# A hand-ordered linear-attention and gated-MLP kernel: three kinds of copies may go to GpSimd, and the written order of all steps is replaced

## The chip, the cores and the metric

The kernel runs on one core of a Trainium2 chip. The metric is the device time of one execution in microseconds (us), as a median of repeated runs; lower is better.

## The reference, cut to what matters

A linear attention with a per-channel decay feeds a gated MLP in float32:

```python
for t in range(S):                       # q, k, v, alpha: (4, 8, 768, 48)
    state = alpha[:, :, t, :, None] * state + np.einsum('bhd,bhe->bhde', k[:, :, t], v[:, :, t])
    y[:, :, t] = np.einsum('bhd,bhde->bhe', q[:, :, t], state)
x = y.transpose(0, 2, 1, 3).reshape(B * S, H * D)      # (3072, 384)
g = x @ w_gate                                         # (384, 1536)
silu = g * (1.0 / (1.0 + np.exp(-g)))
out = (silu * (x @ w_val)) @ w_out                     # (3072, 384)
```

The weights arrive as 64-bit floats.

## The kernel before

**Attention.** The 4 x 768 time steps are cut into 16 units of 192 steps (`u` = 0 to 15; four units are a batch). A unit's loads are alpha, k and q (`La`, `Lk`, `Lq`) and v (`V`). Units 0 to 3 are turned on TensorE (`Ta`, `Tk`, `Tq`, after a widening copy `pa`, `pk`, `pq`), later ones by VectorE's transpose (`tr`, `tk`, `tq`). Then come two scans (`G` backward, `f` forward), k and q multiplied by them (`mk`, `q`), a copy of a part of q (`qc`, line 470, "odd queries") and of v (`vc`, line 476), the scores on TensorE (`S`) and their causal mask on VectorE (`ma`), k turned (`K` with copies `kc` for units 0 to 3, `kr` on VectorE later), the carried state (`B`, or `Bw`, a whole sum with 96 matmul instructions instead of 48), its advance (`ad`), a decay (`de`), and the output (`Y`). Its rows are split in an upper and a lower part (`yh`, `yl`) and moved to the MLP's layout: by TensorE (`R`, `x`) for units 0 and 1, by ten DMAs on the SP queue (`xr`) from unit 2 on.

**MLP.** Eight blocks of 384 tokens, twelve slices of 128 hidden channels each: 96 steps `s`. Each step has three products of nine 128x384 matmuls: `g` (gate), `v` (value) and `o` (out). A float32 product is made of upper and lower parts, so that each factor exists twice. Between them: `sl` (silu, ScalarE, line 700), `h` (times the value product, VectorE, line 704), `hh` (upper part, ScalarE, line 708), `hl` (lower part, line 713, VectorE or GpSimd). There is one PSUM bank for `g` and one for `v`: product `v` of a step starts when `h` of the step before has read the bank. Steps 0 to 6 are block 0, 7 to 13 block 1 (tokens of units 2 and 3), both with the first seven slices.

**Weights.** 19 groups and a last one are loaded as raw 64-bit words (`wl`), cut to float32 by three VectorE operations (`w#v0` to `w#v2`, lines 148, 151, 154), copied as an upper part (`w#a`, line 321) and subtracted for a lower part (`w#p`, line 325). Range checks of all weights follow later (`wr`, `wc`), and those of alpha (`Lc`, `ck`).

**What sets the order.** A string `ORDER` names every step once with its engine: `t` TensorE, `v` VectorE, `s` ScalarE, `g` GpSimd, `y` SP. Each engine runs its own steps in that order, and waits only for the data and the buffers that a step needs. `3+` and `1*` are dummy matmuls on TensorE (lines 766 and 762), which fill waits of the early part. Digits after `@` are PSUM banks.

```python
for word in ORDER.split():
    e, name = word.split(":")
    if name[-1] in "*+":
        (dummy32 if name[-1] == "+" else dummy)(int(name[:-1]))
    else:
        name, *banks = name.split("@")
        todo.pop(name)(engines[e], *(BANKS[int(x)] for x in "".join(banks)))
```

Of the kernel before, what the change touches and what calls it, by code (L numbers as in the profile page):

```python
# [48 lines left out]
s:kc1.0 t:Ta2@45 v:w3v0 s:ad0.2 t:Y0@36 v:q1 y:wl9 v:de1 s:ea2 t:S1@02 v:w4v0 s:yh0.0 v:G2 y:wl10 s:kc1.2 s:vc1 v:w4v1
s:qc1 s:yh0.1 y:wl11 v:w4v2 t:Bw1@1 v:f2 y:wl12 t:Ta3@45 s:ad1.1 v:ma1.1 g:pq2 s:ad1.0 v:ma1.0 v:yl0.1 y:V2 s:ad1.2  # L50
g:pk2 v:yl0.0 v:ma1.2 t:2+ t:Tq2@01 t:R0.1@2 v:w3v1 s:cq2 t:Tk2@36 v:w3v2 s:x0.1 t:Y1@01 v:mk2 g:q2 s:w4a t:R0.0@2
s:yh1.0 t:K2.0@3 s:yh1.1 v:yl1.0 t:K2.2@6 g:w4p s:qc2 v:yl1.1 t:K2.1@0 s:ea3 v:x0.0 t:R0.2@1 y:V3 t:R1.0@2 s:kc2.1
t:S2@45 v:G3 s:x1.0 s:kc2.2 s:kc2.0 t:R1.2@0 v:f3 s:w3a t:R1.1@2 s:x1.2 s:vc2 t:2* t:B2@0 y:Lq3 v:ma2.2 g:w3p s:x1.1
y:La4 s:x0.2 v:ma2.0 t:2* t:g0 v:ma2.1 v:w5v0 y:Lk3 v:w5v1 y:wl13 t:v0 s:sl0 v:w5v2 y:wl14 s:pq3 v:w6v0 t:g1 s:w5a
y:wl15 v:w7v0 v:w6v1 y:wl16 t:Tq3@12 s:sl1 v:w6v2 y:wl17 s:cq3 v:w7v1 s:pk3 v:w7v2 s:w6a y:Lk4 t:2+ t:Tk3@12 v:de2
s:w7a v:mk3 g:w5p v:ad2.0 t:1+ t:2* t:K3.1@1 v:ad2.1 t:K3.2@2 g:w7p s:kc3.1 t:K3.0@3 v:ad2.2 s:kc3.2 y:wl18 v:h0
s:kc3.0 t:2* t:Y2@01 s:hh0 v:de3 v:w8v0 t:v1 s:vc3 y:V4 v:w8v1 s:yh2.0 v:w8v2 s:yh2.1 t:g2 v:yl2.0 g:q3 s:w8a v:h1
v:yl2.1 t:v2 s:hh1 v:hl0 s:qc3 t:S3@01 v:tr4 g:hl1 s:sl2 y:xr2 g:w8p t:g3 v:h2 v:ma3.0 v:tk4 t:Bw3@2 s:sl3 g:w6p
v:ma3.2 v:ma3.1 t:o0 s:ad3.0 v:w9v0 s:ad3.1 v:w10v0 v:w11v0 t:o1 y:La5 s:hh2 v:w11v1 v:w9v1 t:Y3@01 y:Lq4 v:w9v2
v:w10v1 t:v3 s:w9a y:V5 s:yh3.0 v:w10v2 s:vc4 t:g4 v:yl3.0 g:hl2 s:w10a v:h3 v:w9p s:hh3 t:v4 s:sl4 v:w10p s:yh3.1  # L60
t:o2 v:yl3.1 g:hl3 v:h4 y:xr3 v:w12v0 t:o3 v:w12v1 s:hh4 v:w13v0 t:g5 v:w12v2 v:w11v2 t:v5 s:sl5 v:G4 s:w12a t:g6
s:w11a v:h5 g:hl4 s:hh5 t:v6 v:w11p s:sl6 v:w14v0 t:o4 v:h6 g:hl5 v:f4 t:g7 s:hh6 t:v7 s:sl7 v:w14v1 v:w14v2 t:g8 v:h7
g:hl6 t:v8 v:w12p s:sl8 v:w13v1 t:o5 v:h8 v:w15v0 t:o6 v:w15v1 s:hh7 v:w13v2 t:g9 s:hh8 v:w15v2 s:ot6.0 s:ot6.1
y:os6.0 v:mk4 t:v9 s:w14a y:os6.1 v:kr4.0 g:hl7 s:w15a g:hl8 s:sl9 v:kr4.3 s:w13a t:g10 v:kr4.2 g:w13p s:ot6.2 v:kr4.1
s:sl10 t:o7 y:os6.2 g:w14p v:tq4 t:o8 v:h9 y:Lk5 v:w15p t:v10 s:hh9 v:w16v0 v:q4 t:g11 v:w16v1 s:qc4 t:S4@01 v:w17v0
v:w16v2 t:B4@2 v:ma4.2 g:hl9 s:w16a v:h10 g:w16p v:ma4.1 s:sl11 t:v11 s:hh10 v:ma4.0 s:ad4.0 v:tr5 t:g12 g:hl10 y:wl19
v:ad4.1 y:Lq5 t:o9 v:h11 s:sl12 v:G5 t:v12 s:hh11 v:f5 t:g13 v:h12 g:hl11 t:o10 v:tk5 s:sl13 t:v13 s:hh12 v:w18v0
y:La6 v:w18v1 t:g14 v:h13 g:hl12 v:ad4.2 t:o11 s:sl14 v:de5 v:w18v2 t:o12 s:hh13 v:w17v1 v:w17v2 t:Y4@01 v:mk5 s:w18a
# [15 lines left out]
t:o28 s:hh29 v:tk9 g:hl29 t:S8@01 t:B8@2 v:ma8.2 v:f9 t:o29 s:ad8.0 y:La10 t:v30 v:ma8.0 y:Lq9 v:ad8.1 v:ad8.2 t:g31
v:h30 v:de9 s:hh30 t:v31 s:sl31 v:hl30 v:mk9 t:g32 v:h31 v:kr9.1 s:hh31 t:v32 s:sl32 v:kr9.3 t:g33 v:hl31 v:h32
v:kr9.0 t:o30 s:sl33 v:tq9 t:v33 s:hh32 g:hl32 v:kr9.2 y:Lk10 t:g34 v:h33 v:ma8.1 t:o31 v:q9 s:sl34 v:tr10 s:qc9
t:S9@01 s:hh33 t:B9@2 v:G10 y:Lq10 t:o32 v:ma9.0 v:f10 t:v34 t:g35 v:ma9.1 v:h34 v:ma9.2 s:hh34 t:v35 v:hl33 v:hl34
s:sl35 v:ad9.0 t:o33 v:ad9.1 v:h35 t:o34 v:ad9.2 s:hh35 v:hl35 t:g36 v:tk10 t:v36 g:mk10 y:La11 s:sl36 t:g37 v:h36
# [5 lines left out]
t:g43 v:ma10.1 g:hl42 y:wr0 v:kr11.2 y:wr1 t:v43 y:wr2 s:sl43 v:kr11.3 v:ma10.0 t:g44 v:h43 v:f11 t:v44 s:sl44 v:tq11
t:g45 t:o41 v:h44 g:q11 y:Lk12 v:kr11.0 t:o42 v:ad10.0 s:hh43 g:hl43 s:wc0 v:ad10.1 t:v45 v:ad10.2 s:wc1 y:wr3 v:de11
t:o43 s:qc11 v:kr11.1 y:wr4 s:wc2 v:tr12 t:Y10@01 s:sl45 y:wr5 s:hh44 v:h45 g:hl44 y:Lq12 t:g46 v:tk12 s:vc11 s:yh10.0
y:V12 t:v46 v:G12 s:sl46 s:yh10.1 s:hh45 t:g47 v:h46 g:hl45 v:yl10.1 v:yl10.0 t:o44 v:mk12 s:wc3 y:La13 v:f12 t:o45
s:hh46 s:wc4 y:wr6 t:v47 v:tq12 s:wc5 y:wr7 t:S11@01 s:sl47 y:wr8 v:hl46 y:xr10 v:h47 t:B11@2 v:ma11.1 s:hh47 t:g48
# [997 lines left out]
```

## Time and profile before

| | |
|---|---|
| median of 3 runs | 585.48 us (585.07 to 588.24) |
| profiled execution | 588.15 us, span of its instructions 586.4 us |
| TensorE (PE) busy | 557.2 us, 95% of the span |
| VectorE (DVE) busy | 399.4 us, 68% |
| ScalarE (ACT) busy | 256.2 us, 44% |
| GpSimd (POOL) busy | 134.6 us, 23% |
| mean granted TensorE clock | 0.994 |

The span runs from the first to the last instruction; the profiled execution's own time is 1.75 us longer. Busy shares are averages over an early part, in which the attention and the weights are made, and a long part in which TensorE multiplies without a stop.

### The profile page before, as it was taken

The page shows a single profiled execution, that of the slowest core. Times are in us where ns is not written, and L with a number is a line of the kernel's source. Part 1 is how long each engine was busy: PE and PEld are TensorE (multiplying, and loading weights), DVE is VectorE, ACT ScalarE, POOL GpSimd, SP SyncE. Part 2 cuts the span into 40 slices and gives each one's busy share as a digit, 9 for nine tenths or more (in the row PEclk, how much of TensorE's full clock was granted, in tenths as well). Part 3 has the DMA queues.
Part 4 walks back from the last instruction along what each step waited for, and adds up shares of the span by engine and source line. Part 5 has one row for each costly group of instructions (what it writes and reads, how often), then busy time and mean ns, then how long its engine had stood idle before and what let it go on. Part 6 is the DMA issues. An engine that isn't in the chain of part 4 may idle for free.

```text
span 586.4 us, 13722 instructions
## 1 busy us (share of the span) xinstructions
PE 557.2 (95%) x5502; PEld 527.4 (90%) x5502; DVE 399.4 (68%) x625; ACT 256.2 (44%) x591; POOL 134.6 (23%) x130
## 2 busy tenths in 40 slices
...
GB/s 207 292 362 161 312 115 97 40 85 68 144 143 133 122 127 112 122 78 100 87 136 216 193 172 210 227 142 123 220 106 119 72 184 81 60 41 41 0 1 47
DMA packets 95368, 77.67 MB, mean 132 GB/s; under 512 B 32832, under 2 KB 92224, under 8 KB 95296
## 3 DMA queue, kind: packets, MB, share of 16 engines
...
## 4 chain that ended last, share of the span: by engine, by line
PE 69%; DMA 12%; DVE 12%; SPq 3%; issue 3%; ACT 1%; DVEq 0%; ACTq 0%
PE v L692 21%; PE ops L724 21%; PE g L692 21%; DMA raw<-in_moe_w_out_dram 3%; DMA raw<-in_moe_w_gate_dram 3%; DMA raw<-in_moe_w_val_dram 2%; DVE K L505 2%; PE y L619 2%; DVE t L154 1%; PE A L553 1%; DVE h L704 1%; DMA L<-in_q_dram 1%; PE s L530 1%; DMA V<-in_v_dram 1%; DMA Le<-in_k_dram 1%
## 5 line engine op out<-in xcount | busy, mean ns | idle before, releaser
L692 PE MATMUL v<-xT,w 128*128 128x384 f32 x864 | 169.1, 340 | 6.3 <-DVE h L704 6.3
L692 PE MATMUL g<-xT,w 128*128 128x384 f32 x864 | 168.2, 338 | 1.9 <-DMA xT<-X 1.8
L692 PEld LDWEIGHTS v<-xT,w 128*128 128x128 f32 x864 | 151.4, 189 | 9.7 <-DVE h L704 8.8
L724 PE MATMUL ops<-w,hh 128*128 128x384 f32 x576 | 157.8, 337 | 0.0
L692 PEld LDWEIGHTS g<-xT,w 128*128 128x128 f32 x864 | 151.2, 188 | 3.7 <-issue 1.7
L713 POOL TENSOR_TENSOR hl<-h,hh 128x384 fp32r<-128x384 f32 x66 | 73.0, 1108 | 332.1 <-ACT hh L708 327.8
L704 DVE TENSOR_TENSOR h<-h,v 128x384 f32<-128x384 f32 x96 | 53.1, 553 | 115.3 <-PE v L692 108.6
L708 ACT CAST hh<-h 128x384 fp32r<-128x384 f32 x96 | 49.1, 512 | 146.4 <-PE ops L724 85.5
L724 PEld LDWEIGHTS ops<-w,hh 128*128 128x128 f32 x576 | 105.2, 188 | 0.7
L724 PE MATMUL ops<-w,hl 128*128 128x384 f32 x288 | 96.8, 336 | 0.4 <-DVE hl L713 0.4
L700 ACT ACTIVATE h<-g 128x384 f32<-128x384 f32 x96 | 47.0, 490 | 106.4 <-PE g L692 97.3
L505 DVE STREAM_TRANSPOSE K<-Gs 32x384 f32<-32x384 f32 x96 | 54.7, 570 | 2.9 <-PE A L553 1.2
L724 PEld LDWEIGHTS ops<-w,hl 128*128 128x128 f32 x288 | 54.1, 188 | 0.7 <-DVE hl L713 0.7
L713 DVE TENSOR_TENSOR hl<-h,hh 128x384 fp32r<-128x384 f32 x30 | 16.7, 559 | 26.7 <-ACT hh L708 26.4
L448 DVE TENSOR_TENSOR_SCAN AT<-AT,back 128x771 f32<-128x771 f32 x16 | 32.4, 2025 | 0.6
L325 POOL TENSOR_TENSOR w<-t,w 128x768 fp32r<-128x768 f32 (+1 forms) x14 | 26.4, 1903 | 24.0 <-ACT w L321 20.3
L563 DVE TENSOR_TENSOR X<-s,mask 64x384 f32<-64x384 f32 (+1 forms) x48 | 26.2, 553 | 4.2 <-PE s L530 2.9
L439 DVE TENSOR_TENSOR_SCAN Gs<-AT,inj 128x772 f32<-128x772 f32 x16 | 28.2, 1760 | 0.8 <-ACT AT L788 0.6
L297 ACT ACTIVATE wc<-wc,wbias 128x384 f32<-128x384 f32 x36 | 23.4, 650 | 1.2
L321 ACT CAST w<-t 128x768 fp32r<-128x768 f32 (+1 forms) x20 | 15.1, 771 | 17.1 <-DVE t L154 14.8
L154 DVE SCALAR_TENSOR_TENSOR t<-raw,t 128x768 uint32<-128x768 uint32 (+1 forms) x20 | 21.8, 1099 | 0.5
L374 DVE STREAM_TRANSPOSE trq<-L 128x768 f32<-128x768 f32 x12 | 19.5, 1628 | 3.1 <-DMA L<-in_q_dram 2.8
...
## 6 DMA issues: line engine op xcount, KB each, us to landing
...
```

The lines of the kernel that those rows point to most:

```text
L154: lambda: nc.vector.scalar_tensor_tensor(out=t, in0=lo, scalar=29, in1=t, op0=ALU.logical_shift_right, op1=ALU.bitwise_or),
L325: eng.tensor_tensor(out=lo, in0=src, in1=hi.bitcast(F32), op=ALU.subtract)
L439: nc.vector.tensor_tensor_scan(*(x.rearrange("p g t -> p (g t)")[:, ::-1] for x in (Gs, AT, inj)), 0.0, op0=ALU.mult, op1=ALU.add)
L448: nc.vector.tensor_tensor_scan(Af, Af, back[:, 1 : n + 1], back[:, 0:1], op0=ALU.mult, op1=ALU.add)
L505: nc.vector.transpose(out=bass.AP(k0.tensor, k0.offset, [k0.ap[0], (G * 2 * D, NU), (2 * D, G), (1, 32)]), in_=Kg[j * BO + x : j * BO + x ...
L563: nc.vector.tensor_tensor(out=X[r, z, f * GF : (f + 1) * GF, :].rearrange("r g (c t) -> r g c t", c=NU), in0=sps[f][r].rearrange("r g (c t ...
L692: nc.tensor.matmul(pt, wsp[kind, f][a][:, kt * P : (kt + 1) * P], xT[blk][:, b_, kt, :], start=(n == 0), stop=(n == 3 * KT - 1),)
L700: nc.scalar.activation(h, acc.pop(("g", blk, f)), AF.Silu)
L704: nc.vector.tensor_tensor(out=h, in0=h, in1=acc.pop(("v", blk, f)), op=ALU.mult)
L708: nc.scalar.copy(out=hh, in_=acc["h", blk, f])
L713: eng.tensor_tensor(out=hl, in0=acc.pop(("h", blk, f)), in1=hh.bitcast(F32), op=ALU.subtract)
L724: nc.tensor.matmul(ops[blk][i], h[b_][:, i * P : (i + 1) * P], wsp["o", f][a], start=(first and n == 0), stop=(last and n == 2),)
```

## The change

Three kinds of copies that were ScalarE's by their code take their engine from the order now. `ORDER` is another string; it has the same steps, save that the state of unit 2 is carried as a whole sum (`Bw2` for `B2`), and that dummy matmuls are grouped otherwise: 22 of line 766 for 24, 20 of line 762 for 16. Besides ScalarE's copies, steps that could take GpSimd before are dealt out anew. From VectorE to GpSimd go 19 `hl`, 5 `mk`, 5 `q` and 4 `w#p`, from GpSimd to VectorE 18 `hl`, 7 `w#p` and 3 `q`. From ScalarE to GpSimd go 7 `qc`, 4 `vc`, 4 `w#a` and a `pk`, the other way `pq1` and `pk2`; the three `ad2` go from VectorE to ScalarE.

```diff
-y:La0 y:wl0 y:Lq0 y:La1 y:Lq1 y:Lk0 y:V0 s:pa0 t:3+ t:1* t:Ta0@01 v:w0v0 v:w0v1 s:ea0 v:w0v2 v:G0 s:pa1 y:Lk1 s:w0a
+y:La0 y:wl0 y:wl1 y:Lq1 y:La1 y:Lq0 y:Lk0 s:pa0 y:V1 t:3+ t:1* t:Ta0@01 v:w0v0 v:w0v1 s:ea0 v:w0v2 v:w1v0 v:w1v1 s:w0a
...
-        def high(src):
+        def high(eng, src):
...
-            nc.scalar.copy(out=parts[0][:, 0, :], in_=src)
+            (eng.copy if eng is nc.scalar else eng.tensor_copy)(out=parts[0][:, 0, :], in_=src)
...
-    def q_odd(u):
+    def q_odd(u, eng):
         X, r = state[u]["X"], slice(BO, BO + D)
-        nc.scalar.copy(out=X[r, 1, 0:GF, :], in_=X[r, 0, 0:GF, :])
+        (eng.copy if eng is nc.scalar else eng.tensor_copy)(out=X[r, 1, 0:GF, :], in_=X[r, 0, 0:GF, :])
...
-        todo[f"qc{u}"] = lambda eng: q_odd(u)
+        todo[f"qc{u}"] = lambda eng: q_odd(u, eng)
...
-        todo[f"w{p}a"] = lambda eng: wfns[p][1][0]()
+        todo[f"w{p}a"] = lambda eng: wfns[p][1][0](eng)
```

**TensorE, around the first MLP products.** Before, the third product (`g1`) is followed by unit 3's turnings (`pt_2`, `pt_1`) and dummies:

```order
L692 MATMUL g_1_846<-xT_619,w_373 128x384 x9
L394 MATMUL pt_2_0_867<-ident,wide 128x128 x3
L394 MATMUL pt_2_1_871<-ident,wide 128x128 x3
L766 MATMUL early_ps<-inj 128x512 x2
L394 MATMUL pt_1_0_896<-ident,wide 128x128 x3
L394 MATMUL pt_1_1_900<-ident,wide 128x128 x3
L766 MATMUL early_ps<-inj 128x512
L762 LDWEIGHTS inj
L762 MATMUL early_ps<-inj 128x512
```

Now, from the last matmuls of unit 2's output (`y_2`) on:

```order
L619 MATMUL y_2_892<-X_103,V_77 48x64
L692 MATMUL g_0_940<-xT_619,w_168 128x384 x9
L489 MATMUL kps_1_957<-ident,Gs_800 64x112 x4
L692 MATMUL v_0_962<-xT_619,w_173 128x384 x9
L692 MATMUL g_1_982<-xT_619,w_623 128x384 x9
L530 MATMUL s_3_1008<-X_104,Gs_800 64x64 x2
```

Unit 3's turnings, unit 2's output and all dummies have moved ahead of `g0`, and no dummy stands behind it.

**VectorE, around `h3`** (`h_3`; `y_3` with line 637 is `yl3`, `t_` the cutting of a weight group, line 325 its lower part). Before:

```order
L151 SCALAR_TENSOR_TENSOR t_1154<-raw_511,t_1154 128x768
L154 SCALAR_TENSOR_TENSOR t_1154<-raw_511,t_1154 128x768
L637 TENSOR_TENSOR X_104<-y_3_1175,X_104 112x2x192
L704 TENSOR_TENSOR h_3_1131<-h_3_1131,v_3_1219 128x384
L325 TENSOR_TENSOR w_1229<-t_1150,w_1229 128x768
L325 TENSOR_TENSOR w_1254<-t_1154,w_1254 128x768
L637 TENSOR_TENSOR X_104<-y_3_1176,X_104 112x2x192
L704 TENSOR_TENSOR h_4_1270<-h_4_1270,v_4_1260 128x384
```

Now:

```order
L704 TENSOR_TENSOR h_2_1155<-h_2_1155,v_2_1145 128x384
L637 TENSOR_TENSOR X_104<-y_3_1161,X_104 112x2x192
L637 TENSOR_TENSOR X_104<-y_3_1162,X_104 112x2x192
L374 STREAM_TRANSPOSE trk_1243<-L_72 128x4x6x32
L704 TENSOR_TENSOR h_3_1241<-h_3_1241,v_3_1227 128x384
L148 TENSOR_SCALAR t_1279<-raw_761 128x768
L713 TENSOR_TENSOR hl_3_1283<-h_3_1241,hh_3_1277 128x384
```

Both halves of `yl3` stand right behind `h2` now; before, `h3` and two weight groups' lower parts stood ahead of the second half.

**SP, around the ten DMAs of `xr3`** (`xT<-X_104`). Before, the four loads of unit 5's alpha and the four of unit 4's q (of which two are shown) stand in front of v's loads and of `xr3`:

```order
L369 DMA L_71<-in_q_dram 32x4x288
L370 DMA L_71<-in_q_dram 32x4x256
L413 DMA V_78<-in_v_dram 64x4x48 x6
L676 DMA xT_1080<-X_104 48x2x192 x2
L676 DMA xT_1080<-X_104 32x2x192
L676 DMA xT_1080<-X_104 16x2x192
```

Now:

```order
L277 DMA raw_1118<-in_moe_w_out_dram 128x768
L413 DMA V_77<-in_v_dram 64x4x48 x6
L413 DMA V_78<-in_v_dram 64x4x48 x6
L676 DMA xT_992<-X_104 48x2x192 x2
L676 DMA xT_992<-X_104 32x2x192
L676 DMA xT_992<-X_104 16x2x192
```

The loads of alpha and q stand behind `xr3` now, and the loads of units 4 and 5's v directly in front of it.

## Rows read from the trace of the kernel before

**Rows 1.** Four stretches: busy us (and count) of PE, PEld, DVE, ACT, POOL; granted clock; DMA.
```profile
0.00:49.24 49.24, 39.41 (x667) 27.72 (x667) 41.74 (x63) 34.22 (x81) 20.19 (x34) 1.00 0.89 266
49.24:80.13 30.89, 27.20 (x358) 22.78 (x356) 26.88 (x43) 14.30 (x31) 13.58 (x12) 1.00 0.88 232
80.13:130.00 49.87, 43.82 (x324) 41.91 (x320) 45.03 (x57) 17.62 (x34) 16.31 (x11) 0.97 0.32 80
130.00:250.00 120.00, 118.48 (x1237) 113.66 (x1236) 114.17 (x177) 33.74 (x71) 31.55 (x26) 1.00 0.48 121
```

**Rows 2.** Timeline of TensorE, 69 to 87 us: start, us, operation, idle before.
```profile
69.46 1.83 PE L692 MATMUL v<-xT,w 128*128 128x384 f32 x9 [1.18 <-DVE h L704]
...
80.13 1.84 PE L692 MATMUL v<-xT,w 128*128 128x384 f32 x9
...
85.09 1.83 PE L692 MATMUL v<-xT,w 128*128 128x384 f32 x9 [1.55 <-DVE h L704]
```

**Rows 3.** Waits of VectorE from 0 to 72.3 us: total, times, longest.
```profile
DVE t L148 <- DMA raw<-in_moe_w_val_dram: 2.1, 1, 2.1
DVE Gs L814 <- PE pt L394: 1.8, 1, 1.8
```

**Rows 4.** Timeline of VectorE and, last, of GpSimd, 38 to 73 us.
```profile
38.51 2.40 DVE L154 SCALAR_TENSOR_TENSOR t<-raw,t 128x768 uint32<-128x768 uint32 x1
...
56.20 0.96 DVE L154 SCALAR_TENSOR_TENSOR t<-raw,t 128x768 uint32<-128x768 uint32 x1
...
71.74 0.53 DVE L704 TENSOR_TENSOR h<-h,v 128x384 f32<-128x384 f32 x1
...
38.42 1.68 POOL L464 TENSOR_TENSOR X<-trq,AT 112x768 f32<-112x768 f32 x1 [3.04 <-ACT trq L788]
```

**Rows 5.** Groups by form: count, busy us, mean ns of one, idle before.
```profile
L325 DVE TENSOR_TENSOR w<-t,w 128x768 fp32r<-128x768 f32 x5 | 4.7, 947 | 0.0
L713 DVE TENSOR_TENSOR hl<-h,hh 128x384 fp32r<-128x384 f32 x30 | 16.7, 559 | 26.7 <-ACT hh L708 26.4
L148 DVE TENSOR_SCALAR t<-raw 128x768 uint32<-128x768 uint32 x16 | 11.1, 709 | 0.1
L374 DVE STREAM_TRANSPOSE AT<-L 128x768 f32<-128x768 f32 x12 | 19.5, 1625 | 0.2
L580 DVE TENSOR_TENSOR V<-A,V 48x192 f32<-48x192 f32 x46 | 16.3, 354 | 1.1
L713 POOL TENSOR_TENSOR hl<-h,hh 128x384 fp32r<-128x384 f32 x66 | 73.0, 1108 | 332.1 <-ACT hh L708 327.8 <-DVE AT L374 4.3
L817 POOL TENSOR_TENSOR Gs<-trk,Gs 128x768 f32<-128x768 f32 x4 | 6.8, 1689 | 22.1 <-DVE trk L374 17.9 <-DVE Gs L439 4.2
L382 POOL COPY wide<-L 128x576 f32<-128x576 f32 x3 | 3.8, 1279 | 13.7 <-issue 6.0 <-DMA L<-in_k_dram 5.0 <-PE pt L394 2.7
```

**Rows 6.** Timeline of TensorE, 97 to 105 us.
```profile
97.69 0.68 PE L692 MATMUL g<-xT,w 128*128 128x384 f32 x3
...
100.95 1.30 PE L692 MATMUL g<-xT,w 128*128 128x384 f32 x3 [1.37 <-DMA xT<-X]
...
104.66 0.51 PE L692 MATMUL g<-xT,w 128*128 128x384 f32 x2
```

**Rows 7.** Timeline of the SP queue, 88 to 100 us.
```profile
88.14 4.10 SPq L413 DMA_DIRECT2D V<-in_v_dram  x6
92.35 6.84 SPq L676 DMA_DIRECT2D xT<-X  x10
```

**Rows 8.** Timeline of TensorE, 121 to 129 us.
```profile
121.07 1.83 PE L692 MATMUL v<-xT,w 128*128 128x384 f32 x9 [1.74 <-DVE h L704]
...
127.23 1.83 PE L692 MATMUL v<-xT,w 128*128 128x384 f32 x9 [0.84 <-DVE h L704]
```

**Rows 9.** Timeline of TensorE, 18 to 20 us.
```profile
18.79 1.28 PE L553 MATMUL A<-V,K 128*48 128x48 f32 x48
```

**Rows 10.** The chain that ended last, in order of time: start, us, what.
```profile
159.49 1.57 PE ops L724 x9
```

More of the change, by code (lines that the diff above doesn't have):

```diff
@@ L49 @@
[L49 to L68, printed above, removed]
@@ L84 @@
[L84 to L88, printed above, removed]
@@ L94 @@
[L94 to L98, printed above, removed]
@@ new lines @@
+v:w1v2 v:G0 s:w1a y:Lk1 s:pa1 y:La2 s:pq0 t:4+ t:Ta1@01 v:w1p y:Lk2 t:Tq0@23 v:f0 s:pk0 y:V0 t:1* t:Tk0@45 s:pq1 v:q0
+g:pk1 g:w0p v:mk0 t:1+ t:3* t:Tk1@23 s:ea1 y:Lq2 s:ek1 t:1* t:Tq1@45 v:G1 y:La3 t:S0@01 y:wl2 s:qc0 y:wl3 t:K0.0@2
+s:pa2 t:K0.2@3 v:f1 s:kc0.0 t:K0.1@6 y:Lk3 s:vc0 y:wl4 s:kc0.1 y:wl5 v:ma0.2 g:mk1 s:kc0.2 t:1+ t:2* t:Ta2@26 s:pa3
+y:wl6 t:Bw0@1 v:w2v0 s:cq1 v:w2v1 y:wl7 v:w2v2 g:q1 t:K1.2@3 v:ma0.0 s:ad0.1 t:K1.1@4 t:K1.0@5 v:ma0.1 s:kc1.2 y:wl8
+s:kc1.1 v:w3v0 s:qc1 t:4* t:S1@34 v:w3v1 s:ad0.2 v:w3v2 y:wl9 s:ea2 v:de1 s:ad0.0 t:1+ t:3* t:Ta3@02 v:G2 s:kc1.0
@@ new lines @@
+t:Tq3@13 g:w4p s:ad2.0 s:ad2.1 v:ma2.1 v:ma2.0 v:w7v0 s:ad2.2 v:w7v1 y:wl15 t:Y2@02 v:w7v2 s:cq3 v:de3 s:w7a y:wl16
+t:g0 v:f3 s:yh2.0 s:yh2.1 s:vc3 t:K3.1@1 t:v0 y:wl17 s:sl0 v:yl2.0 g:q3 s:kc3.1 v:yl2.1 t:g1 y:xr2 v:h0 s:hh0 v:w7p
+s:qc3 t:S3@01 v:w5v2 s:sl1 t:K3.2@2 v:ma3.2 g:hl0 t:K3.0@3 s:w5a t:v1 v:ma3.1 s:kc3.0 v:ma3.0 s:w6a v:w5p t:o0 s:kc3.2
+v:w8v0 v:w6p t:Bw3@0 v:h1 v:w9v0 s:hh1 v:w10v0 y:wl18 t:g2 v:w10v1 s:ad3.0 s:ad3.1 v:w8v1 y:V4 t:v2 s:sl2 v:w8v2
+v:w9v1 s:w8a t:Y3@01 v:w9v2 t:g3 v:w8p s:w9a y:V5 s:yh3.0 v:w11v0 s:yh3.1 v:h2 g:hl1 v:yl3.0 t:v3 s:hh2 g:w9p v:yl3.1
@@ new lines @@
+s:sl3 v:tk4 t:o1 y:xr3 g:hl2 v:h3 t:g4 s:hh3 v:w12v0 s:vc4 v:hl3 v:w12v1 t:v4 s:sl4 v:w12v2 t:g5 v:h4 v:w11v1 t:o2
+s:sl5 v:w11v2 y:La4 v:w10v2 s:w12a t:o3 s:hh4 v:w12p y:La5 s:w10a t:v5 v:hl4 s:w11a v:w10p t:o4 v:w13v0 v:w13v1 t:g6
+v:w13v2 v:h5 g:w11p s:w13a t:v6 s:sl6 v:tr4 s:hh5 g:hl5 t:g7 v:h6 y:Lq4 v:w14v0 s:hh6 t:v7 v:w15v0 s:sl7 v:w15v1 t:o5
+v:w13p v:h7 g:hl6 t:g8 s:hh7 v:w14v1 t:o6 v:w14v2 s:sl8 v:w15v2 s:w14a t:v8 s:ot6.0 v:w16v0 s:ot6.1 y:os6.0 v:w16v1
+y:os6.1 t:g9 v:h8 g:hl7 s:hh8 v:w16v2 t:v9 s:sl9 v:hl8 s:w16a v:G4 t:g10 s:ot6.2 y:os6.2 t:o7 v:f4 s:sl10 t:o8 v:h9
```

137 lines of the change are left out of this document (76 added, 61 removed).

## The prediction

> **What bounds the kernel.** I read the busy table first, then stretches of it, then TensorE's timeline, then what VectorE and the SP queue did at each of its gaps. TensorE is busy for 95% of the span, so only its idle time can be won, or work taken from it. By stretches [rows 1] it idles 49.24 - 39.41 = 9.8 us before the first MLP product (`g0`, at 49.24), 3.7 us from there to the start of the fourth value product (`v3`, at 80.13 [rows 2]), 6.1 us from there to 130, and 1.5 us in the 120 us after that. The busy time before `v1` also holds the dummies. So what can be won lies nearly all in the first 130 us, and there the engine to look at is VectorE: in the stretches from 49.24 on it is busy 87%, 90% and 95% of the time, and TensorE's gaps in front of `v2` (1.18 us), `v4` (1.55) [rows 2], `v10` (1.74) and `v11` (0.84) [rows 8] all end with line 704, the `h` that must read the value bank first. One gap is another's: `g7`, the first product of block 1, waits for `xT`. It starts at 97.69, `v7` follows, and `g8` starts at 104.66 [rows 6]: 7.0 us for two products that take 1.57 each at the pace of a product in the chain [rows 10], so 3.8 us are lost, to the wait and to the clock (0.97 on average in that stretch [rows 1]). The ten DMAs that bring unit 3's rows there start at 92.35 and take 6.8 us to issue, behind 4.1 us of v's loads [rows 7].
>
> **Step 1: the way to `v3`.** `v3` is a good mark, since TensorE has nearly the same to do before it in both orders. Read off the two orders, it gains the longer carry of unit 2 (48 more instructions, at most 1.28 us, as the row with 48 of them [rows 9]) and loses `o1`, which now follows (1.57 us); of the dummies two dear ones go and four cheap ones come, which I count as even. All dummies, the turnings of unit 3 and the output of unit 2 now stand ahead of `g0`, where TensorE idled 9.8 us; before, they stood between `g1` and `v1`. So `v3` moves by the waits alone. What holds it is `h2`: it frees the bank, and the new order leaves just the output of unit 3 and one product between `v2` and `v3`. Before, `h2` ran at 71.74 to 72.27 [rows 4]. VectorE's steps ahead of `h2`, old list against new: it is rid of `w0p`, `hl0` (0.56 us each), `mk1`, `q1` (0.95 each), `tr4` (1.63) and the eight adds of `ad2` (at most 0.354 each): 7.5 us. It takes on `w1p`, `w2p`, three masks `ma3` (0.56 each), `w5p` to `w8p` (four of 0.95), three first cuts (0.71) and three later ones (0.96): 11.6 us [rows 4, 5]. Neighbours overlap by some 0.08 us, so I take the net as +4. Against that stand two waits of VectorE ahead of `h2`, together 3.9 us [rows 3]. The 2.1 us wait is for the raw words of the first value weights, whose load was the tenth step of the SP queue and is the third now. The 1.8 us wait is for `Tk3`, which TensorE now does ahead of `g0`. With both gone `h2` ends at 72.3 + 4 - 3.9 = 72.4, with both kept at 76.3. `v3`, at 80.13 before, then comes 3.8 to 7.7 us earlier. I take 5: new waits on GpSimd come in, since `mk1` and `q1` are on the chain to unit 1's scores and take 1.69 us there [rows 5] instead of 0.95. Below, nothing is certain: the idle time ahead of `g0` has a chain of its own (rival 1), so the bound is 0.
>
> **Step 2: `v4`.** Before, eight cuts stood between `h2` and `h3`. Now both halves of `yl3`, `tk4` and `h3` follow `h2`: 0.56 x 2 + 1.63 + 0.55 = 3.3 us, while TensorE does `v3`, `o1` and `g4` (4.7 us). The 1.55 us go; I take -1.5 (0 to -1.55).
>
> **Step 3: `g7`.** `yl3` ends 1.1 us behind `h2`, that is at 73.5 to 77.4. Then v's loads (4.1 us) and `xr3` (6.8 us, and some 2 us to land, since the last DMA was issued at 99.2 and the last third of `g7` started at 100.95 [rows 6, 7]) make 86.4 to 90.3. `g7` stands eleven products behind the start of `v3`, 17.3 us, so at about 92 where I put `v3` at 75, and at 89.7 at the earliest. That fits. If it does not, the eight loads now behind `xr3` are not what was in its way. I take -3.5 (0 to -3.8).
>
> **Step 4: `v10`, `v11`.** Between `h8` and `h9` stood four cuts, `mk4`, eight transposes of unit 4's k and `tq4`; now one cut, `hl8` and the two scans of unit 4. The gaps were 1.74 + 0.84 = 2.6; I take -2 (0 to -2.6).
>
> **Step 5: what is added.** `o1`, now behind `v3`: +1.6. The same work on GpSimd takes twice as long: an `hl` 1.11 against 0.56 us [rows 5]. Summed by rows, GpSimd gets one `hl` more (1.1), five `mk` (8.4), two `q` net (3.4 at the same 1.7), three `w#p` fewer (-5.7 at 1.9, twice VectorE's), seven `qc`, four `vc`, four `w#a` and one wide copy fewer. No copy of these shapes ran on GpSimd. By its copy of 576 columns at 1.28 us [rows 5], 2.2 ns a column, a `qc` (384) takes 0.85, a `vc` (2 x 288) 1.3 and a `w#a` (768, one of 384) 1.7 or 0.85: 17.1, less 1.3. Bounds: nothing dearer than a two-input operation of 768 columns (1.69), nothing cheaper than VectorE's rate for 768 columns (0.95). In all some +23 us on an engine that is busy 23%; ScalarE and VectorE lose about 7 us each. Nobody waits for it as long as each result has its cover: an `hl` has two products of 1.57 us or more before its `o`. If the cover is gone, a step costs its whole length, 1 to 2 us. I take +0.5 for the part after 130 us (-1.5, the idle time there, to +4).
>
> **Sum.** -5 - 1.5 - 3.5 - 2 + 1.6 + 0.5 = -9.9 us, on a span of 586.4 and an execution of 588.15. The median of the runs, 585.48, is 0.5% below that execution; I subtract the same from it: **575.6**.
>
> **A rule against the change.** The row: a cut that takes 0.96 us alone took 2.40 while a GpSimd multiplication of 1.68 us ran beside it [rows 4], 0.86 us lost for each us of GpSimd; `h`, with one input in PSUM, kept 0.53. [...] The price goes by the row, as rival 2.
>
> **Rivals.** (1) *The early chain isn't VectorE's.* Ahead of `g0` TensorE idles on several engines in turn, so step 1 may bring only 0 to 1, step 2 nothing and step 4 half; step 3 stays: -1 - 3.5 - 1 + 1.6 + 0.5 = -3.4, 582. For it: `mk1` and `q1` get slower; against: 3.9 us of named waits lose their cause. (2) *GpSimd slows VectorE.* VectorE has 120 - 114.2 = 5.8 us to spare from 130 to 250 us [rows 1]. If half of the 23 us falls there at 0.86, it loses 10; the 4.2 us above the spare reach TensorE: 575.6 + 4.2, about 580. Against: the 7 us it is rid of. (3) *Slower: late `hl`.* Nine `o` now follow their `v` by two or three products with the `hl` on GpSimd (`o0`, `o32`, `o41`, `o45`, `o54`, `o55`, `o74`, `o75`, `o77`). The way is `h` 0.55, `hh` about as much, `hl` 1.11, so 2.2 us, within 3.1; behind a 1.7 us copy it is 3.9. If each stalls by 1.4 us, nine make 12.6: 588. It decides from 1.1 us each, where they eat the whole gain.
>
> **Chances.** Forecast 0.64 (its own range 570 to 580), rival 1 0.16, rival 2 0.11, rival 3 0.06, better than the forecast's range 0.03. Best case of all bounds: -7.7 - 1.55 - 3.8 - 2.6 + 1.3 - 1.5 = -15.9, 569.6. The range is 569.6 to 583.5; it leaves out rival 3 and the edge of rival 1. A measurement tells about 0.5% from no change: below 582.6 is faster (0.64 + 0.03, rival 2, most of rival 1: 0.86), above 588.4 slower (0.05), else same (0.09).
>
> **What would show it.** Right: `v3` near 75, no idle of over 1 us before `v4`, `v10`, `v11`; `xr3` issued before 85 and `g7` without an `xT` wait; no dummy behind `g0`. Wrong: TensorE idle by 10 us or more before `g0` with `g0` past 57 (step 1); VectorE's cuts or scans over 1.5 us in most places (rival 2); TensorE waiting for line 713 (rival 3).

## The result, and the profile after

The changed kernel took 580.1 us (median of 4 runs, 577.86 to 581.99) beside 586.86 for the kernel before on the same chip: a ratio of 0.9876, with a 95% interval of 0.9838 to 0.9913. It is faster, by 1.2%. The profiled execution took 579.38 us with a span of 577.7 (588.15 and 586.4 before). TensorE is busy for 97% of the span.

Marks on TensorE tell where the 8.7 us came from. These are starts in the two profiles, in us; `o95` is the last product.

| | `g0` | `v3` | `v10` | `v11` | `o95` | from `v11` to `o95` |
|---|---|---|---|---|---|---|
| before | 49.24 | 80.13 | 121.07 | 127.23 | 577.20 | 449.97 |
| after | 60.11 | 79.90 | 115.86 | 120.65 | 568.46 | 447.81 |

Up to `v3` the change brings 0.2 us, from there to `v11` 6.4, and behind `v11` 2.2. The timeline of TensorE after shows it (columns as in [rows 2]):

```profile
37.02 0.33 PE L394 MATMUL pt<-ident,wide 128*128 128x128 f32 x1 [0.68 <-DVE Y L637]
37.97 0.76 PE L394 MATMUL pt<-ident,wide 128*128 128x128 f32 x5 [0.63 <-issue]
...
39.68 0.37 PE L602 MATMUL y<-X,V 128*64 128x64 f32 x1 [0.35 <-ACT SE L578]
...
54.86 0.39 PE L553 MATMUL A<-V,K 128*48 128x48 f32 x8 [2.42 <-issue]
...
57.15 0.37 PE L602 MATMUL y<-X,V 128*64 128x64 f32 x1 [1.10 <-ACT SE L578]
...
79.90 1.83 PE L692 MATMUL v<-xT,w 128*128 128x384 f32 x9 [1.30 <-DVE h L704]
...
84.70 1.72 PE L692 MATMUL v<-xT,w 128*128 128x384 f32 x9
...
96.77 1.86 PE L692 MATMUL v<-xT,w 128*128 128x384 f32 x9 [0.97 <-DVE h L704]
98.47 1.72 PE L692 MATMUL g<-xT,w 128*128 128x384 f32 x9
...
115.86 1.82 PE L692 MATMUL v<-xT,w 128*128 128x384 f32 x9
...
381.17 1.85 PE L692 MATMUL v<-xT,w 128*128 128x384 f32 x9 [0.52 <-DVE h L704]
```

The waits of [rows 2, 6, 8] in front of `v4`, `g7`, `v10` and `v11` are gone; `v6` (96.77) has a new one of 0.97 us. In the early part stand gaps that the order before did not have there, and the windows show what came with two of them (columns as in [rows 1]):

```profile
39.61:43.02 3.41, 3.30 (x73) 2.85 (x74) 3.38 (x7) 0.96 (x4) 0.00 (x0) 0.50 1.00 222
...
52.43:56.67 4.24, 1.19 (x15) 0.90 (x14) 3.45 (x6) 1.32 (x5) 1.80 (x1) 1.00 1.03 362
56.67:60.09 3.42, 2.94 (x72) 2.70 (x72) 2.81 (x5) 2.56 (x7) 0.00 (x0) 0.50 1.09 305
...
79.90:130.00 50.10, 49.12 (x363) 48.20 (x364) 46.77 (x58) 17.87 (x35) 20.29 (x17) 1.00 0.37 90
130.00:250.00 120.00, 120.00 (x1315) 116.13 (x1314) 110.00 (x176) 30.27 (x64) 41.06 (x38) 1.00 0.49 120
```

For 3.41 us twice, behind the idle spells at 36 to 39.7 and at 52.4 to 57.2 (TensorE busy for 2.0 of 3.7 us and for 1.3 of 4.8), the granted clock was 0.50; the outputs `Y1` and `Y2` fell into it and took 3.33 and 3.04 us, where `Y0` took 1.76.

From 80 us on TensorE idles 1.0 us in 50, and not at all from 130 to 250 (6.1 and 1.5 us before, [rows 1]).

VectorE's `h2` frees the bank for `v3`. Timeline of VectorE after at `h0`, then the windows up to the end of `h2`, of the changed kernel and of the one before:

```profile
64.03 0.55 DVE L704 TENSOR_TENSOR h<-h,v 128x384 f32<-128x384 f32 x1 [2.23 <-PE v L692]
```

```profile
0.00:79.85 79.85, 69.49 (x1062) 52.54 (x1062) 67.75 (x100) 50.82 (x119) 25.85 (x43) 0.96 0.87 250
```

```profile
0.00:72.27 72.27, 58.75 (x875) 43.35 (x876) 62.47 (x97) 46.26 (x105) 29.83 (x43) 1.00 0.91 266
```

`h2` ended 7.6 us later than before: ahead of it VectorE was busy for 5.3 us more (67.75 beside 62.47) and idle for 2.3 us more (12.1 beside 9.8).

### The profile page after: what moved, and what is told of

It is laid out like the page before. It is cut to its first block, busy times and chain, and to the rows that moved or that the text cites. A ratio compares the mean times of both kernels' runs of the same rounds, so it can differ in the third digit from the quotient of the medians.

```text
span 577.7 us, 13799 instructions
## 1 busy us (share of the span) xinstructions
PE 558.3 (97%) x5552; PEld 529.9 (92%) x5552; DVE 391.6 (68%) x612; ACT 249.5 (43%) x581; POOL 148.9 (26%) x153
## 4 chain that ended last, share of the span: by engine, by line
PE 82%; DVE 8%; DMA 6%; SPq 1%; issue 1%; ACT 0%; DVEq 0%; ACTq 0%
PE v L692 25%; PE ops L724 25%; PE g L692 24%; DMA raw<-in_moe_w_val_dram 2%; PE y L619 2%; DMA L<-in_k_dram 2%; PE A L553 2%; PE s L530 2%; DVE t L151 2%; DVE AT L448 1%; PE y L602 1%; PE y L603 1%; DVE Gs L439 1%; DMA raw<-in_moe_w_gate_dram 1%; DMA xT<-X 1%
## 5 line engine op out<-in xcount | busy, mean ns | idle before, releaser
L708 ACT CAST hh<-h 128x384 fp32r<-128x384 f32 x96 | 49.0, 512 | 152.4 <-DVE h L704 76.3
L505 DVE STREAM_TRANSPOSE K<-Gs 32x384 f32<-32x384 f32 x96 | 54.7, 570 | 5.5 <-PE A L553 3.8
L448 DVE TENSOR_TENSOR_SCAN AT<-AT,back 128x771 f32<-128x771 f32 x16 | 34.3, 2144 | 0.7
L713 DVE TENSOR_TENSOR hl<-h,hh 128x384 fp32r<-128x384 f32 x29 | 16.0, 556 | 15.9 <-ACT hh L708 15.8
L464 POOL TENSOR_TENSOR X<-trq,AT 112x768 f32<-112x768 f32 x11 | 18.9, 1716 | 27.7 <-ACT trq L788 12.8
L325 POOL TENSOR_TENSOR w<-t,w 128x768 fp32r<-128x768 f32 (+1 forms) x11 | 19.1, 1742 | 22.2 <-ACT w L321 21.9
L553 PE MATMUL A<-V,K 64*48 64x48 f32 (+1 forms) x720 | 21.4, 207 | 2.4 <-issue 2.4
L817 POOL TENSOR_TENSOR Gs<-trk,Gs 128x768 f32<-128x768 f32 x9 | 15.4, 1707 | 28.5 <-DVE trk L374 14.6
```

Of the source, the lines that this page charges most:

```text
L448: nc.vector.tensor_tensor_scan(Af, Af, back[:, 1 : n + 1], back[:, 0:1], op0=ALU.mult, op1=ALU.add)
L505: nc.vector.transpose(out=bass.AP(k0.tensor, k0.offset, [k0.ap[0], (G * 2 * D, NU), (2 * D, G), (1, 32)]), in_=Kg[j * BO + x : j * BO + x ...
L553: nc.tensor.matmul(to[j * BO : j * BO + D, g - gs.start, :], Ks[r, x, g, KC[j]], Vd[r, x, g, VC[j]], start=(x == 0 or not whole), stop=(x ...
L708: nc.scalar.copy(out=hh, in_=acc["h", blk, f])
L713: eng.tensor_tensor(out=hl, in0=acc.pop(("h", blk, f)), in1=hh.bitcast(F32), op=ALU.subtract)
```

## The experiments

Each row of this table is a profiled execution (starts in us) and the ratio of its runs to the kernel before on the same chip, with the 95% interval. The changed kernel's own runs spread from 577.9 to 582 us, so intervals here are some 0.4% to either side. The marks tell better where time went, but each is one execution's: the profiled one took 2.9 us more than the median of its runs in warm (580.44 beside 577.57), 2.7 us more in xr3b and 1.8 us less in warmsp. What a change is worth at the end has to be weighed by both.

The expectations speak of three theories. Theory 1: TensorE's own chain from 36 to 60 us held `v3`, by the half clock and the gap inside `Bw2`. Theory 2: VectorE's early chain held it. Theory 3 came up in the run with dummies: behind an early `v3`, the SP queue holds `v10`.

| run | `v3` | `v10` | `v11` | `o95` | ratio |
|---|---|---|---|---|---|
| changed kernel | 79.90 | 115.86 | 120.65 | 568.46 | 0.9876 (0.9838 to 0.9913) |
| again | 79.50 | 115.45 | 120.25 | 568.04 | 0.9869 (0.9826 to 0.9911) |
| xr3b | 80.48 | 116.40 | 122.55 | 576.46 | 0.9953 (0.9921 to 0.9985) |
| b2 | 80.30 | 117.41 | 122.28 | 570.35 | 0.9833 (0.9788 to 0.9878) |
| warm | 76.41 | 116.01 | 120.81 | 568.55 | 0.9823 (0.9774 to 0.9873) |
| wl2 | 77.78 | 115.32 | 120.19 | 568.16 | 0.9827 (0.9783 to 0.9871) |
| sp | 79.47 | 116.17 | 120.96 | 568.69 | 0.9850 (0.9801 to 0.9899) |
| warmsp | 75.88 | 112.59 | 117.46 | 565.08 | 0.9839 (0.9795 to 0.9883) |
| all | 77.03 | 113.70 | 118.52 | 566.35 | 0.9823 (0.9783 to 0.9864) |
| mkq | 78.24 | 114.18 | 118.97 | 566.75 | 0.9857 (0.9826 to 0.9889) |
| act | 81.69 | 117.66 | 122.45 | 570.28 | 0.9859 (0.9827 to 0.9891) |
| eng | 76.65 | 113.47 | 118.15 | 567.70 | 0.9891 (0.9850 to 0.9933) |
| best | 76.24 | 112.95 | 117.75 | 565.57 | 0.9832 (0.9801 to 0.9864) |

**The changed kernel again** (no edit).

> The changed kernel itself once more, beside the three that follow: how far the two half-clock spells (39.6 and 56.7 us) and the gap inside Bw2 (2.4 us) come back in a second profile. Theory 1 needs them to come back, in place if not in size; if they are an accident of one execution, g0 is at 57 or earlier here. Ratio 0.984 to 0.990.

The gap inside `Bw2` came back with 2.15 us and `Y1` and `Y2` took 3.33 and 3.03 us (granted clock 0.52 and 0.55 over 3.41 us). So they are no accident of one execution. But the first half-clock spell does not always come: in mkq and eng `Y1` ran at a clock of 1.00 (2.16 us), in mkq behind idle times of 0.68, 0.71 and 0.35 us, where this run has 0.68, 0.82 and 0.35; and in b2 and wl2 the mean clock of the first 60 us was 0.96 and 0.97, beside 0.94 in the changed kernel and here, as with one spell in place of two. What decides it, no run here shows. The marks repeat within 0.5 us.

**Unit 2's short carry** (b2).

```diff
-t:Bw2@6 ... s:ad2.0 s:ad2.1 ... s:ad2.2
+t:B2@6 ... v:ad2.0 v:ad2.1 ... v:ad2.2
```

> The changed order, but with unit 2's carry short again (B2, 48 matmul instructions, for Bw2's 96) and its three advances on VectorE. Theory 1 (what cancelled step 1 is TensorE's own chain from 36 to 60 us: two spells at half clock and a 2.4 us gap inside Bw2): the gap shrinks or goes, the carry takes 1.3 us in place of 5.0, Y2 runs in 1.8 us, g0 starts 3 to 5 us earlier than 60.1 and v3 2 to 4 us earlier than 79.9; the time falls by 2 to 4 us, a ratio of about 0.982 to the kernel before. Theory 2 (VectorE's early chain holds v3): VectorE gets eight more adds, 2.5 us, ahead of h2; v3 starts at 80 to 82.4, and the ratio is 0.988 to 0.992.

The gap went, and another took its place. Timeline of TensorE, then a window:

```profile
56.37 0.34 PE L602 MATMUL y<-X,V 128*64 128x64 f32 x1 [4.22 <-DVE SE L580]
```

```profile
57.00:61.00 4.00, 4.00 (x71) 3.73 (x68) 3.90 (x6) 2.16 (x5) 0.00 (x0) 0.50 1.11 251
```

`Y2` now waits 4.2 us for the advances, which VectorE comes to late, and the half clock follows that idle time as well (`g0` took 3.04 us). The run tells the theories apart badly: both had a part of it right.

**Dummies in the idle places** (warm).

```diff
-t:Tk2@14 ... t:Y1@35 ... t:Y2@02
+t:3* t:Tk2@14 ... t:1* t:Y1@35 ... t:2+ t:Y2@02
```

> The changed order with dummies in three idle places of TensorE: three small ones ahead of Tk2, one ahead of Y1, two large ones ahead of Y2. Theory 1: the granted clock stays at full in one or both places, Y1 or Y2 take 1.8 us in place of 3.3 and 3.0; for each, g0 and v3 come about 1.3 to 1.6 us earlier, v3 at 77 to 78.5, ratio 0.983 to 0.986. Theory 2: g0 comes earlier, v3 stays within 0.5 us of 79.9, ratio 0.988. If the two large dummies only delay Y2, by up to 0.5 us, v3 is later by as much.

From 36 to 60 us the clock is 1.00, `Bw2` runs through in 2.37 us (an "issue" gap of 1.53 us stands among the dummies at 36.9 instead), `Y2` takes 1.76, and `v3` starts at 76.41, 3.5 us earlier. So theory 1 holds for `v3`. VectorE has no wait any more from 54.7 us to `h2`, that for `v0` included, so its own work sets `v3` here. But `v10` and `o95` stand where they stood in this profile. Timelines of TensorE, VectorE and ScalarE in this run:

```profile
84.93 1.83 PE L692 MATMUL g<-xT,w 128*128 128x384 f32 x9 [1.96 <-ACT h L700]
95.24 1.83 PE L692 MATMUL v<-xT,w 128*128 128x384 f32 x9 [0.66 <-DVE h L704]
99.64 1.83 PE L692 MATMUL v<-xT,w 128*128 128x384 f32 x9 [1.00 <-DVE h L704]
116.01 1.82 PE L692 MATMUL v<-xT,w 128*128 128x384 f32 x9 [0.41 <-DVE h L704]
```

```profile
97.62 1.58 DVE L374 STREAM_TRANSPOSE AT<-L 128x768 f32<-128x768 f32 x1 [2.43 <-POOL hl L713]
```

```profile
82.03 0.43 ACT L476 COPY U<-V 64x288 f32<-64x288 f32 x1 [1.64 <-DMA V<-in_v_dram]
83.94 0.43 ACT L476 COPY U<-V 64x288 f32<-64x288 f32 x1 [1.47 <-DMA V<-in_v_dram]
```

Four waits of 4.0 us in all stand between `v3` and `v10`, where the changed kernel has one of 0.97. `sl4` stands behind `vc4` on ScalarE, which waits for V4; `tr4` waits for unit 4's alpha (the profile names `hl` there, but in the run warmsp `tr4` follows `h5` at once). Both loads come off the SP queue, which in the changed kernel issues from 65.44 us on without a pause (compare [rows 7]):

```profile
65.44 9.65 SPq L676 DMA_DIRECT2D xT<-X  x10
...
76.37 9.36 SPq L413 DMA_DIRECT2D V<-in_v_dram  x12
85.83 6.54 SPq L676 DMA_DIRECT2D xT<-X  x10
92.46 0.53 SPq L369 DMA_DIRECT2D L<-in_alpha_dram  x1
```

In the run with dummies the same rows start at 65.97, 76.44, 86.17 and 92.80: the queue did not move with TensorE. That gave theory 3. The timed runs do not bear out that nothing is won at the end: this profiled execution is the slowest but one of its six, and their ratio is 0.9823, where the changed kernel has 0.9876 and 0.9869 (the intervals overlap).

**The third weight group's load earlier** (wl2).

```diff
-y:V0 ... y:wl2
+y:wl2 y:V0 ...
```

> The changed order with the load of the third weight group (wl2) ahead of unit 0's v loads on the SP queue. VectorE waited 2.6 us for that group's raw words. Theory 1: the wait shrinks or goes, VectorE waits elsewhere instead, g0 and v3 stay within 0.5 us, or are later where unit 0's v is now late for the first scores' carry; ratio 0.988. Theory 2: h2 and v3 come 2 to 2.6 us earlier, v3 at 77.3 to 78, ratio 0.984.

VectorE's wait of 2.6 us went, and `v3` came 2.1 us earlier, as theory 2 said, but on theory 1's way: `g0` came 2.2 us earlier too (57.87), since TensorE's outputs and turnings there wait for VectorE, and the mean clock of the first 60 us was 0.97, 0.94 in the changed kernel: one half-clock spell less. I put that at 1.2 of the 2.1 us, an estimate from `Y1`, which took 2.16 us at a clock of 1.00 in mkq and 3.33 in the changed kernel. So the two theories name two links of one chain. The end did not move here either (`o95` at 568.16).

**xr3 and La4 ahead of V4 and V5** (sp), and with the dummies (warmsp).

```diff
-y:V4 ... y:V5 ... y:xr3 s:vc4 ... y:La4 ... s:sl6 ... y:Lq4
+y:xr3 y:La4 y:V4 ... s:sl6 s:vc4 ... y:Lq4 y:V5
```

> The changed order, on the SP queue xr3 and La4 ahead of V4 and V5, and on ScalarE vc4 behind sl6; nothing in the first 75 us moves. Theory 3 (an earlier v3 is swallowed before v10 by what SP issues without a break from 65.4 to 96.3 us, and by vc4, which waits for V4): here, with v3 where it was, only the 0.6 us wait of tr4 and a part of v6's wait go; v3 at 79.9, v10 0.5 to 1.5 us earlier than 115.9, ratio 0.986. Rival (VectorE's own work between h2 and h9 holds v10): v10 within 0.3 us of 115.9.

> The dummies of the run before (v3 at 76.4, v10 still at 116.0) together with the new places of xr3, La4, V4, V5 and vc4. Theory 3: g5 does not wait for sl4 (2.0 us before), tr4 does not wait for its alpha (2.4 us), and v10 starts 3 to 4 us earlier, at 112 to 113; the time falls by as much against the run with dummies alone, ratio about 0.977. Rival (VectorE's own work holds v10): v10 stays at 115 to 116, ratio 0.982.

Alone the edit brings nothing (`v10` at 116.17, so the 0.5 us that I expected at the least did not come, and the rival's sign did). From `v3` to `v10` it even takes 36.7 us, where the changed kernel takes 36.0, with a new wait of 0.53 us in front of `v10`. With the dummies, `v10` starts at 112.59, 3.4 us earlier than with dummies alone, and `o95` 3.5 us earlier. Timelines of TensorE, SP and VectorE of warmsp:

```profile
75.88 1.85 PE L692 MATMUL v<-xT,w 128*128 128x384 f32 x9 [1.30 <-DVE h L704]
...
82.27 1.72 PE L692 MATMUL g<-xT,w 128*128 128x384 f32 x9
...
112.59 1.85 PE L692 MATMUL v<-xT,w 128*128 128x384 f32 x9 [0.55 <-DVE h L704]
```

```profile
76.36 7.17 SPq L676 DMA_DIRECT2D xT<-X  x10
83.63 0.53 SPq L369 DMA_DIRECT2D L<-in_alpha_dram  x1
```

```profile
92.19 0.55 DVE L704 TENSOR_TENSOR h<-h,v 128x384 f32<-128x384 f32 x1
92.65 1.67 DVE L374 STREAM_TRANSPOSE AT<-L 128x768 f32<-128x768 f32 x1
```

`g5` (82.27) and `tr4` do not wait any more. So in the profiles theory 3 holds: an earlier `v3` comes through to `v10` where SP's queue moves with it. The run mkq below fits: its `v3` and its `o95` came earlier by as much, and its queue had moved by itself (`xr2` issued from 63.15 and unit 4's alpha from 89.99, where the changed kernel has 65.44 and 92.46). The timed runs do not show it. I expected a ratio of 0.977; it came out at 0.9839, beside 0.9823 with the dummies alone.

**All three** (all: the edits of warm, wl2 and sp together).

> Dummies, the earlier load of the third weight group, and the new places on SP together. Theory 3 with both theories of the early part: v3 at 74 to 75.5 (the load's 2 us and the dummies' 3.5 us overlap), v10 at 110.5 to 112, ratio 0.974 to 0.977. If VectorE is what is left between v3 and v10, v3 comes at 75 and v10 no earlier than 112.

`v3` came at 77.03, 1.5 to 3 us later than expected and 1.2 later than in warmsp. `S1` started only at 27.69 (25.60 in warmsp): TensorE waited 1.9 us at 22.8 for copies of unit 0's k, which stand on ScalarE behind `vc0` and its wait for V0; in warm and wl2 this wait was 0.9 us. Whether the earlier load delays V0, or the first loads just landed later in this execution, one profile does not tell. From `v3` on the run goes as warmsp does. The ratio of 0.974 to 0.977 that I expected did not come either (0.9823), but timed it is the clearest of all: its six runs (575.86 to 577.57 us) lie below all six of the changed kernel that ran beside them on the same chip (again, 578.38 to 581.02).

**The step of the queue alone** (xr3b, an edit of the kernel before).

```diff
-y:La5 ... y:Lq4 ... y:xr3
+y:xr3 y:La5 y:Lq4
```

> The kernel before, with the eight loads of unit 5's alpha and unit 4's q behind xr3 on the SP queue in place of ahead of it: step 3 alone. If step 3 is right: xr3 is issued from about 88.3 in place of 92.35, g7 does not wait for xT, the half-clock spell at 100.9 is gone, the start of g8 comes 3 to 3.8 us earlier against v3, and the time falls by about 3.5 us, ratio 0.994. Rival (another thing is in the way of xr3, or the time is given back later): g8 moves by less than 1 us, or the ratio stays at 1.000.

`g7` does not wait, `g8` starts at 99.98 instead of 104.66, and `v11` is 4.7 us earlier: 3.8 us from this wait and the clock, 1.2 from `v4`, whose wait is 0.36 here, less the 0.35 that `v3` is later. But `o95` is only 0.7 us earlier. Timelines of TensorE and VectorE, and a window, of this run:

```profile
96.86 1.72 PE L692 MATMUL g<-xT,w 128*128 128x384 f32 x9
...
99.98 1.75 PE L692 MATMUL g<-xT,w 128*128 128x384 f32 x9
...
381.94 0.44 PE L724 MATMUL ops<-w,hl 128*128 128x384 f32 x1 [2.30 <-DVE hl L713]
```

```profile
376.16 1.64 DVE L374 STREAM_TRANSPOSE trq<-L 128x768 f32<-128x768 f32 x1 [5.33 <-DMA L<-in_q_dram]
```

```profile
382.20:386.50 4.30, 4.30 (x17) 4.30 (x17) 4.16 (x10) 1.54 (x5) 0.00 (x0) 0.60 0.68 217
```

TensorE arrives 4.7 us early at a place where a load of q does not: VectorE waits 5.3 us for it (2.5 before), an `hl` behind it comes 2.3 us late, and the clock falls for the next product. There the order before takes 4 of the 4.7 us back, in this execution. The timed runs keep more: their ratio of 0.9953 makes 2.8 us of the 3.5 that I expected. In the order after TensorE waits at that place for 0.52 us (the row at 381.17 above), and nowhere else between 130 us and `o95`.

**mk1 and q1 on VectorE** (mkq).

```diff
-g:mk1 ... g:q1
+v:mk1 ... v:q1
```

> The changed order with unit 1's two multiplications (mk1, q1) on VectorE in place of GpSimd. [...] v3 0 to 2 us earlier than 79.5 to 79.9; time within 0.5% of the changed kernel, ratio 0.984 to 0.988.

Timeline of VectorE and, last, of GpSimd in the changed kernel, then of VectorE in this run:

```profile
17.59 3.19 DVE L448 TENSOR_TENSOR_SCAN AT<-AT,back 128x771 f32<-128x771 f32 x1
...
24.45 2.00 DVE L151 SCALAR_TENSOR_TENSOR t<-raw,t 128x384 uint32<-128x384 uint32 x1
...
17.48 1.69 POOL L817 TENSOR_TENSOR Gs<-trk,Gs 128x768 f32<-128x768 f32 x1 [1.77 <-DVE Gs L439]
24.35 1.68 POOL L464 TENSOR_TENSOR X<-trq,AT 112x768 f32<-112x768 f32 x1 [5.18 <-ACT trq L788]
```

```profile
17.34 1.82 DVE L448 TENSOR_TENSOR_SCAN AT<-AT,back 128x771 f32<-128x771 f32 x1
...
24.30 0.56 DVE L151 SCALAR_TENSOR_TENSOR t<-raw,t 128x384 uint32<-128x384 uint32 x1
```

A window of this run, over `Y1`:

```profile
38.97:41.13 2.16, 1.97 (x73) 1.69 (x74) 2.13 (x5) 0.92 (x3) 0.00 (x0) 1.00 1.21 232
```

The scan loses 1.37 us and the cut 1.44 to their neighbours on GpSimd, and get them back when these go. `S1` did not come earlier (26.46; it waits for `q1` behind the cuts), but `v3` did, by 1.3 to 1.7 us, and `o95` by as much. Of this, 1.2 us are the clock's: `Y1` ran at 1.00 and took 2.16 us where it had taken 3.33. And with the dummies, where the mean clock of the first 60 us is 1.00 (warmsp and best), the same edit brings `v3` no earlier (best, below). So the collisions are shown, but not that they cost `v3` anything.

**The new copies back on ScalarE** (act), **and every step on its old engine** (eng).

```diff
-g:w2a g:qc2 g:w15a ... (15 copies)
+s:w2a s:qc2 s:w15a ...
```

> The changed order with all 15 copies that are GpSimd's by the new freedom (seven qc, four vc, four w#a) back on ScalarE. If the order alone carries the gain: the same marks as the changed kernel, v3 at 79.5 to 80, v11 at 120 to 121, o95 447.8 us after v11, ratio 0.985 to 0.989; GpSimd's busy time falls by about 10 us. If the copies' freedom matters: ScalarE's steps behind them (kc, sl, hh) come late and o95 is 1 us or more later against v11.

> The changed order with every step on the engine that it had before (79 steps moved back: hl, mk, q, w#p and the copies; unit 2's advances stay on ScalarE): the order without the new dealing. If the order alone carries the gain: v11 within 1 us of 120.5, o95 447.8 us after v11, ratio 0.985 to 0.990. If the dealing carries it: TensorE waits for lines 704 or 713 in several places after 130 us, o95 3 us or more later against v11, ratio 0.992 or more.

With the copies on ScalarE GpSimd is busy 136.9 us instead of 148.9, and the way from `v11` to `o95` is 447.83 us, as it was: the new freedom as such brings and costs nothing that these runs can tell. (`v3` is 1.8 us later there; the mean clock was 0.92 from 60 to 80 us, where `g0` runs, and 1.00 in the changed kernel.) With all 79 steps back, the way from `v11` to `o95` is 449.55 us, 1.7 longer, in pieces of at most 0.46 us; that is most of the 2.2 us that the change gains there. Ahead of `v11` the old dealing is 2.1 to 2.5 us quicker in the profile, with `f1` and `f4` alone on VectorE (`f4` took 2.04 us, 3.35 in the changed kernel), but also with `Y1` and `Y2` at a clock of 1.00 (2.16 and 1.76 us), which alone is worth 2.5 us and which no edit of this run aims at. In the timed runs the two add up to no difference that stands out. Neither forecast fits eng as it stands (`v11` is 2 us earlier, `o95` 1.7 us later against it). So the order carries the gain up to `v11`, and 1.7 of the 2.2 us behind it come with the dealing.

**Dummies, SP and mk1, q1** (best: the edits of warm, sp and mkq together).

> Dummies and the new places on SP (run with v3 at 75.9 and v10 at 112.6) and mk1, q1 on VectorE. If GpSimd's share costs VectorE 1.3 us net there: v3 at 74 to 75.5, v10 at 111 to 112.3, end of the span at 573 to 574, ratio 0.978 to 0.983. If not: v3 and v10 as in that run or up to 1.5 us later.

`v3` at 76.24 and `v10` at 112.95 are 0.4 us later than in warmsp: with the dummies, mk1 and q1 gain nothing more. The 1.3 us net of the expectation were my estimate, and no run shows them: in mkq the scan and the cut got 2.81 us back, and `mk1` and `q1` took 0.95 us each on VectorE. The profiled span ends at 574.8 us, at 574.1 in warmsp, against 577.7 and 577.4 of the changed kernel. Timed, best is at 0.9832 and warmsp at 0.9839 beside 0.9876 and 0.9869: surely faster than the kernel before, and probably than the changed one, but the intervals overlap.

## Why the prediction held, and where it failed

The direction and the range were right (569.6 to 583.5, measured 580.1), the forecast 4.5 us too low. Of these, 1.1 us are the sum's: -9.9 from 588.15 makes 578.25, and the profiled execution took 579.38. The other 3.4 us are the step from there to the median: I took off 0.5%, as the median before lay below its profiled execution, but beside the changed kernel the median before was 586.86, and the changed kernel's own median lies 0.7 us above its profiled execution. One profiled execution does not say on which side of the median the next one falls.

The sum itself came close by luck, since its misses cancelled in part: step 1 brought 4.8 us less than its term, step 5 2.7 us more, and steps 2 to 4 with `o1` 1.0 us more. The measured time is also the one that rival 2 gave (about 580), without its mechanism. And the bounds are looser than they look: the best case counts `o1` at 1.3 us where the sum has 1.6, and no sum is given for the upper bound of 583.5.

**Step 1 failed**: -0.2 us for `v3` instead of -5. The sentence that failed is "So `v3` moves by the waits alone. What holds it is `h2`." `v3` did wait for `h2`, but the two waits that were to leave VectorE's way, 3.9 us, had successors: its idle time ahead of `h2` grew by 2.3 us, and its busy time by 5.3 where I had 4. From `h0` to `h2` VectorE indeed runs without a pause for 15.8 us; but `h0` waited 2.2 us for `v0`, so what set the start was TensorE. There the dear term was the one that I had put at 1.28 us or less: `Bw2` took 5.0 us against the 1.28 of a short carry, 1.3 for its 48 more instructions and 2.4 for a gap; the half clock added 1.6 at `Y1` and 1.3 at `Y2`. In the run with dummies the clock stays at 1.00 and no gap falls into `Bw2` (one of 1.53 us stands at 36.9 instead), and `v3` comes 3.5 us earlier, at 76.4, at the late edge of the 72.4 to 76.3 that I had worked out. The rest stays open. A wait of 2.6 us for a weight group took the place of the 2.1 us wait in [rows 3], and GpSimd slowed two operations of VectorE; but taking these away (wl2, mkq) gained in part by the clock, and beside the dummies neither brought `v3` earlier (77.03 in all, 76.24 in best, 75.88 without them). What I named as the sign of a failure, `g0` past 57 with 10 us of idle time ahead of it, is nearly what the profile shows (60.11 and 9.1 us): rival 1 was right on step 1, though not on steps 2 and 4, which it held to depend on it.

**Steps 2 to 4 were right.** The waits of 1.55 us at `v4`, 3.8 at `g7` and 2.6 at `v10` and `v11` are gone. With `o1` (+1.57), the new wait at `v6` (+0.97), and `o9` ahead of `v11` in place of `S4` and `B4` (-0.5), they make -5.9; 6.4 were measured, and a product that need not start after a wait is some 0.1 us shorter (1.72 instead of 1.83). Step 3 alone on the kernel before is confirmed up to `v11`, but there the profile gives its gain back at 380 us, and the timed runs a part of it. In the changed kernel it is kept. Steps 2 and 4 are read off the profiles; no run takes them alone. One term of step 3 was too small: 4.1 us for v's loads is the price of six, and the new order has twelve there, which took 9.36 us, so that `xr3` was issued from 85.83 to 92.37. With some 2 us to land, that is late for a `g7` at 92, where I had put it (in warm, with an early `v3`, it was issued to 92.70 all the same); it was in time since `g7` came at 98.47.

**Step 5 had the wrong sign**: -2.2 us behind `v11` instead of +0.5. GpSimd's share rose by 14.3 us, not by 23, for more than half because its copies were cheaper (12.0 us by the run act, where I had put 17.1); and no product waits for line 713, so rival 3 did not come. Rival 2's price was right where it applied (1.37 and 1.44 us lost beside operations of 1.69 and 1.68: 0.81 and 0.86 for each us), but after 130 us VectorE kept 10 us in 120 free.

**And if step 1 had come true, the end need not have moved.** I had put `v3` and `v10` as terms to be added. In the profile of the run with dummies they are not: with `v3` at 76.4 the loads behind `xr2` on the SP queue set `v10`. How much of that the timed runs share is open (their ratio is no worse than with the queue changed).
